# Finer DMA transposes of q and k, ten x buffers and attention further ahead in a fused attention and MLP kernel

## The chip, the cores and the metric

One core of a Trainium2 chip. The metric is the time of one execution on the device in microseconds (us), as the median of several runs. PE is the matmul engine, PEld its weight loads, DVE the vector engine, ACT the scalar engine, POOL the engine that issues the loads, SP the engine whose queue issues the DMA transposes and the stores.

## The reference

```python
def _attn_ref(q, k, v):                      # q, k, v: [8, 8, 576, 64]
    scores = scale * q @ k.T                 # per batch and head
    mask = (rel >= 0) & (rel < 128)          # sliding window, ALiBi bias
    attn = softmax(where(mask, scores + bias, -1e9))
    return attn @ v
def _moe_ref(x, w_in, w_out):                # x: [4608, 512]
    h = x @ w_in                             # [4608, 2048]
    return (h * cos(h)) @ w_out              # [4608, 512]
```

The output of the attention, with heads joined, is the `x` of the second part.

## The kernel before

Attention is cut into 72 units: per batch eight units (head pair `pr`, token half `G`) and a tail unit `t`. The second part is cut into nine chunks of 512 tokens. Each chunk has a first stage (64 matmuls of 512 columns, in two of the chunks 128 of 256) and a second stage, which from chunk 1 on is made of seven products instead of eight. Between the stages of chunk c, `QUOTA[c]` units of attention are worked.

```python
QUOTA = [9, 9, 11, 11, 9, 9, 5]
NX = 8                                        # x buffers
...
def dma_transposes(b):                        # batches 2 to 7, on the SP queue
    for which in ("q", "k"):
        fns = [ ...transpose of token blocks 0 to 3..., ...transpose of the tail block... ]
        op("sp", fns, r=[("nat", which, b % 2)] + ..., w=[("tr", which, b % 2)], ...)

def load_nat(which, src, b):                  # q or k of a batch, on the POOL queue
    op("pool", fns, r=[("tr", which, 0)] if b == 3 else [], w=[("nat", which, b % 2)], ...)

def tkeys(u):                                 # what the scores of a unit wait for
    keys = [("tr", w_, b % 2) for w_ in ("q", "k")] + [("ktail", b % 2)]
```

The `r=` of `load_nat` for batch 3 holds the q loads of that batch until the q transposes of batch 2 have landed, and the k loads likewise for k. Each finished x tile is transposed either by PE or, when its chunk is not the next one, by DMA from the SP queue:

```python
first = (S * u[0] + (512 if u[1] == "t" else 256 * u[2])) // CH
by_dma = first > phase + 1
```

A string `STARTS` holds a planned start for each operation, worked out beforehand; operations are sorted by it, and each engine runs its own in that order. Stores of the result go through four buffers `ob` and stand in the same SP queue as all transposes by DMA:

```python
op(("act", "dve"), ..., w=[("B", bank), ("ob", oi), ...])                      # PSUM to ob
op("sp", [lambda e: e.dma_start(out[row:row + 128, :], ob[oi])], r=[("ob", oi)], ...)   # the store
```

The softmax here doesn't subtract the row's maximum and nothing guards it: scores larger than these inputs give would overflow.

## Time and profile before

| | kernel before |
|---|---|
| median of the first 3 runs | 301.37 us (301.10 to 301.57) |
| the profiled run | 302.63 us, span 300.9 us |
| PE busy | 291.0 us of the span |
| PE idle from 20 to 290 us | 2.60 us |
| DVE, ACT, POOL busy | 80%, 70%, 32% |

The row to read first is the last but one: if PE is the bound, its idle time in the middle is all that a change of waits can win. The profile is of one run, and that run was 1.3 us slower than the median. The lines themselves stand in the prediction.

### The profile page before, as it was taken

The numbers are of one execution on the slowest core, as the hardware profiler recorded it, in microseconds if no ns is written. First come the engines' busy times: TensorE is split into PE (matmuls) and PEld (weight loads), VectorE is DVE, ScalarE is ACT, GpSimd is POOL, SyncE is SP. The second block draws the span as 40 slices with busy tenths as digits, with TensorE's granted clock in tenths as the row PEclk, the third lists the DMA queues.
The fourth block names the chain that finished last, engine by engine and source line by source line (L and its number), as shares of the span: only waits on it lengthen the run. The fifth ranks groups of instructions, "written<-read, shape, count | busy, mean of one in ns | idle before, by whom it ended". The sixth has DMA issues, their size and how long they took to land.

```text
span 300.9 us, 7105 instructions
## 1 busy us (share of the span) xinstructions
PE 291.0 (97%) x2905; PEld 200.6 (67%) x2925; DVE 240.5 (80%) x478; ACT 209.7 (70%) x300; POOL 95.2 (32%) x122
## 2 busy tenths in 40 slices
PE   7799999999999999999999989999999999999996
PEld 3568746547774687548888876568755855566685
DVE  4687678789977998899988879788978967685871
ACT  6787977498857788588768775778676945645432
POOL 7998230069966322760196004000000000000000
PEclk9999999999999999999999999999999999999999
DMA  7999999999999999999999999942304111120033
GB/s 140 181 199 210 206 166 174 140 167 172 172 132 138 173 153 163 145 193 140 184 114 126 148 128 137 170 87 64 98 21 105 46 27 52 37 75 32 0 124 122
DMA packets 148352, 38.09 MB, mean 127 GB/s; under 512 B 133984, under 2 KB 147040, under 8 KB 148320
## 3 DMA queue, kind: packets, MB, share of 16 engines
q0 software_dynamic: 99344, 18.10, 78.4%
q1 hardware_dynamic: 48976, 19.54, 37.9%
q8 instruction: 23, 0.38, 0.5%
q14 instruction: 9, 0.07, 0.1%
HBM read 36.70 MB, written 9.44 MB: 153 GB/s over the span
## 4 chain that ended last, share of the span: by engine, by line
PE 59%; DMA 21%; POOL 14%; SPq 3%; issue 2%; DVE 0%; ACT 0%; POOLq 0%; DVEq 0%; ACTq 0%
PE ps L768 27%; PE ps L909 26%; DMA qnat<-in_q_dram 8%; DMA knat<-in_k_dram 7%; POOL vp L329 4%; POOL qnat L339 4%; SPq L350 3%; DMA qt<-qnat 3%; DMA kt<-knat 3%; PE ps L538 3%; POOL knat L339 2%; PE ps L623 1%; PE ps L626 1%; POOL w_outb L367 1%; POOL w_inb L361 1%
## 5 line engine op out<-in xcount | busy, mean ns | idle before, releaser
L768 PE MATMUL ps<-xT,w_inb 128*128 128x512 bf16 (+1 forms) x556 | 125.2, 354 | 0.7
L774 ACT ACTIVATE cos<-ps,halfpi 128x512 f32<-128x512 f32 x128 | 82.4, 687 | 46.2 <-PE ps L768 34.8
L778 DVE TENSOR_TENSOR gT<-ps,cos 128x512 f16<-128x512 f32 x128 | 83.0, 686 | 21.6 <-ACT cos L774 21.1
L768 PEld LDWEIGHTS ps<-xT,w_inb 128*128 128x128 bf16 x576 | 55.2, 98 | 39.7 <-DVE xnat L679 0.8
L568 ACT ACTIVATE p<-ps 128x768 bf16<-128x768 f32 (+1 forms) x64 | 55.6, 917 | 9.3 <-PE ps L538 8.5
L329 POOL DMA_DIRECT2D vp<-in_v_dram x40 | 34.0, 871 | 61.8 <-PE ps L626 48.1
L909 PE MATMUL ps<-wsum,gT 128*128 128x256 f16 x256 | 50.8, 273 | 0.4
L592 DVE TENSOR_TENSOR p<-p,emask 128x512 bf16<-128x512 bf16 (+2 forms) x88 | 39.0, 471 | 4.0 <-ACT p L568 3.5
L909 PE MATMUL ps<-w_outb,gT 128*128 128x256 f16 x256 | 39.7, 273 | 0.1
L909 PE MATMUL ps<-wsum,gsum 128*128 128x256 f16 x256 | 37.2, 273 | 0.1
L339 POOL DMA_DIRECT2D qnat<-in_q_dram x30 | 25.4, 892 | 18.1 <-DMA qt<-qnat 17.3
L909 PEld LDWEIGHTS ps<-wsum,gT 128*128 128x128 f16 x256 | 24.2, 98 | 9.1 <-DVE ob L933 0.8
L909 PEld LDWEIGHTS ps<-w_outb,gT 128*128 128x128 f16 x256 | 24.5, 98 | 8.4 <-ACT ob L929 0.3
L339 POOL DMA_DIRECT2D knat<-in_k_dram x30 | 25.6, 919 | 8.5 <-issue 5.9
L909 PEld LDWEIGHTS ps<-wsum,gsum 128*128 128x128 f16 x256 | 24.7, 98 | 4.6 <-ACT qrows L929 0.2
L909 PE MATMUL ps<-w_outb,gsum 128*128 128x256 f16 x128 | 26.1, 273 | 0.1
L679 DVE TENSOR_TENSOR xnat<-ps,rec 128x512 bf16<-128x512 f32 x28 | 19.3, 690 | 1.3
L929 ACT ACTIVATE qrows<-ps 128x512 f32<-128x512 f32 (+1 forms) x18 | 9.9, 552 | 14.2 <-PE ps L909 14.1
L538 PE MATMUL ps<-qt,kt 64*128 64x128 bf16 (+1 forms) x320 | 18.4, 239 | 1.3 <-issue 0.9
L623 PE MATMUL ps<-vp,p 128*128 128x65 bf16 x256 | 18.0, 193 | 0.8 <-DVE xT L740 0.4
L623 PEld LDWEIGHTS ps<-vp,p 128*128 128x128 bf16 x256 | 15.6, 97 | 3.9 <-issue 1.1
L626 PE MATMUL ps<-vp,p 128*128 128x65 bf16 x192 | 16.9, 193 | 0.0
(81 smaller groups left out, 333.1 us busy)
## 6 DMA issues: line engine op xcount, KB each, us to landing
out_dram<-ob SPq DMA_DIRECT2D x32, 256.0 KB, 4.7
vp<-in_v_dram POOLq DMA_DIRECT2D x32, 128.0 KB, 10.0
qnat<-in_q_dram POOLq DMA_DIRECT2D x24, 128.0 KB, 13.0
knat<-in_k_dram POOLq DMA_DIRECT2D x24, 128.0 KB, 17.4
w_inb<-in_moe_w_in_dram POOLq DMA_DIRECT2D x4, 512.0 KB, 10.2
w_outb<-in_moe_w_out_dram POOLq DMA_DIRECT2D x4, 512.0 KB, 21.9
out_dram<-ob SPq DMA_DIRECT2D x8, 128.0 KB, 1.8
qrows<-in_q_dram POOLq DMA_DIRECT2D x1, 576.0 KB, 15.0
```

What stands on the lines that cost most here:

```text
L329: op("pool", [lambda e, t=t, rows=rows: e.dma_start(vp[b % 2][0:rows, t, :, 0:64], v[b, :, 128 * t:128 * t + rows, :].rearrange("h p d -> ...
L339: fns.append(lambda e, t=t, rows=rows: e.dma_start(nat[which][b % 2][0:rows, t, :, :], src[b, :, 128 * t:128 * t + rows, :].rearrange("h p ...
L538: ins = e.matmul(ps[:, banks[x], c0:c1], keys_ap(b, x, pr, kc), query_ap(b, x, pr, qb, 128 * nb), start=not added, stop=True, skip_group_c ...
L568: op("act", lambda e: e.activation(P[i][:, :, 0:hi], src_[:, :, 0:hi], ACTF.Exp, scale=0.125), w=held + [("P", i)], occ=920 if G else 691, ...
L592: op("dve", lambda e, p=p, m=m: e.tensor_tensor(p, p, m, ALU.mult), r=[("P", i), ("EM", h0), ("EM", h1)], w=[("P", i)] if n != 1 else [("P ...
L623: ins = e.matmul(o, P[i][:, x, d0:d0 + 128], V[:, kc, h, 0:65], start=True, stop=not two)
L626: ins = e.matmul(o, P[i][:, x, p0:p0 + 128], V[:, kc - 1, h, 0:65], start=False, stop=True)
L679: op("dve", lambda e: e.tensor_tensor(o, U[:, :, :, 0:64], rv[:, :, :, None].broadcast_to([128, 2, 4, 64]), ALU.mult), r=[("rec", n // 2 % ...
L768: op("pe", lambda e, kc=kc, c0=c0: e.matmul(ps[:, bank, c0:c0 + n], w_in[:, kc, 128 * fc:128 * fc + 128], xT[:, kc, (r0 + c0) % XR:(r0 + c ...
L774: op("act", lambda e: e.activation(cosb[ci][:, :], ps[:, bank, :], ACTF.Sin, bias=halfpi[:, 0:1]), r=["halfpi"], w=[("B", bank), ("cos", c ...
L778: op("dve", lambda e: e.tensor_tensor(gT[gi][:, fc, :], ps[:, bank, :], cosb[ci][:, :], ALU.mult), r=[("cos", ci)], w=[("B", bank), ("g", ...
L909: op("pe", lambda e, t=t, fc=fc, bk=bk: e.matmul(ps[:, bk, 256 * t:256 * t + 256], lhs(fc, t), rhs(fc), start=first and fc == 0 and (last ...
```

## The change

Its intent is to let the scores of a unit start when the q and k blocks that this unit reads have been transposed, instead of waiting for the whole batch; to work some attention earlier (two units move from the phase of chunk 5 into that of chunk 4, and two from the last phase into that of chunk 5), with two more x buffers for it; and to use other PSUM banks for one early group of transposes. All starts were planned anew. The core of the diff:

```diff
 STARTS = ( ...the whole packed order is replaced... )
-        NX = 8
+        NX = 10
-        QUOTA = [9, 9, 11, 11, 9, 9, 5]
+        QUOTA = [9, 9, 11, 11, 11, 9, 3]
 # load_nat
-            op("pool", fns, r=[("tr", which, 0)] if b == 3 else [], ...
+            op("pool", fns, r=[("tr", which, 0, "p", 1)] if b == 3 else [], ...
 # dma_transposes: one operation of two DMAs for q and one for k become
+            for part, (c0, c1) in enumerate(((0, 2), (2, 4), (4, 5))):
+                for which in ("k", "q"):
+                    ...
+                    op("sp", [lambda e, o=o, i=i: e.dma_start_transpose(o, i)], ...
+                       w=[("tr", which, b % 2, "p", part)], dma=f"tr{which}{b % 2}{part}", ...)
 # tkeys
+            if b >= BPE:
+                parts = {0: {"q": (0,), "k": (0,)}, 1: {"q": (1,), "k": (0, 1)},
+                         None: {"q": (2,), "k": (1, 2)}}[G]
+            keys += [("tr", w_, b % 2, "p", i) for w_ in ("q", "k") for i in parts[w_]]
 # transposes of q of batch 1 by PE
-                    qk_transposes(1, "q", 0, half, SB[2:4])
+                    qk_transposes(1, "q", 0, half, SB[0:2])
```

More of the change, by code (lines that the diff above doesn't have):

```diff
@@ L30 @@
 STARTS = (
-    "c-pO24RBP|72cOXa(x5(I4W)~i!PU!n68h_l0Nn)ci$#JvTT>Qh5<sb{46Q06ag_HP0@nHLTijMGE9d;#FQ$-pI~Q%qT-BFY"
-    "cW#GD1!*tv9_RN!730;7P7DBy<IjxyHU&ZC42Y0bI-l^obP<++_eaL+;Z(nNjm=Fn{E-hvv26ov#utlbwS5Rz**D4Fw`x*pT"
-    "UBV^`+(7ocZasXYy75rdI*~@V_gyWw)jG2H!=pWYA@ZG2>cuRv5@Gp1~`N9uu;Y?k8>az8(mA2LG}y8DnmDmXKv07aJt#!dG"
-    "b#T<xzIe5LQZkY(xYtI59Ro!-mSxEWTr8CvgIy<c2?HTnQ!iXs`~y*B9S7z<ffg|CyW=^i*+18UL~@&1aev~36X#RmzN9m|L"
-    "h%0hq4uNR*Te9$uty#ng)CCAJ(4T>9B33!wc6NG+o_j|YGbpG$)WnW3t#QL$Tub(~45lmS~VkM;6q-!h#Xs|qVQ?F;LQ&eUp"
@@ L36 @@
-    "8dP`6COh6EW2X=jSr<AJSf!WD_3$c9A@paOklWGUCbu)g`n3Kfq;x`WXN7NEo9XHPj%$TXf$2T?3WgK8U-wWc7Ef8`=obc?T"
-    "XdRv64G7j?$5+QSH3*~mT#-$tengJO$K#lWTGX>#O}1+GHZkZ>)346i3_dgP8=LJ&>7s7GRwBaQgT*zSE53MEB_DDr9FdU{j"
-    "0GLyUkFNcXK9KdhEYTfeHf`XtJC40y$X@F>{5Wr`25iI#`jW$oV?0mv^OM)HOgq?(UWG-nmX$3IpGSee{AEwh;T)tLM6|t2E"
-    "?<^rF9<=4>xF(cZWmu4#JYc(1aEe`APoOIExO=~M2<Q+^BAzSI1Rr?tim8eAXGfJHn5U{yu>`?oQfna`Ic1qF8NvYf3s(e1J"
-    "DA4)zHOAc-M4Scrk@ldEN6xvebYB{>~Y^`Iq{>5y)cD(<lGW}FpS((2C2b>RuR@c2}eXYiJXwmKaXTl+vl7A+!oY|a=%_)*P"
@@ L41 @@
-    "1HKXG3(v8R+{ny#JW{7TY(&?nyMvD{TR8pHc=?!gxBV@-U7ku8d-gn%-%`Ma16?JZ*8Z&y2Qo{At=e8jL_*xu%105=FM=di@"
-    "jnA99e}zUP+)|JRz6G;32H>^<Z&tiLW$^{JkqulP!<FHY1~6R>D^w!|49rxLW=oZAhLw>RNIUyQV5l|^S?>72F(5Tp&ca+RO"
-    "TIM9f%Oc$|r_Oq5<DLw`+?>zZ#95XkRjvZL{s1_2gKXI(n4TJCXWtE|Mx_n;IHhIKu-KOmc^PQJU?OD)K9Q;Ot&+;HAAEsw{"
-    "~b(%X+8w?`W&tC0X|K$U{kAOS0m19b#g<044~30(y59NS4iaiLd|gED*bkz0bHdWIUPUhZyV;AUs-f#PCRFuo5YHK4sv6LdH"
-    "6iPdjP0quU7v>xX_T-dgW@hiCHiqh4%XQ1?Hrouv=hbPFsH7cI_(+8m%!ka%deDKXhpUNwK8$?;V6P;k=S8w%tF9wg(w}O+$"
@@ L46 @@
-    "z$Dq_^iHPsQ7Go;6^DyH|CI-o!ynzh!?oTJN00M>oNqItta{zsFyr;t+m1#*cYTQ98VNNA5Q+8OdlQnBROj(ZT9q=A@ne075"
-    "M>%QM6sDr5DWGjNez{Vvdu`PXd8Q`&?z!e^5PN-wKg~1HS&NVV(LX{1#t(8>4cJlDlo?9)>F#(%W4ZW@hLIZxJ|oA)cR)Lv3"
-    "<F^llvG{Gd_C(Kvb&$rr3E=HH8V<?->O<UkuU$#=l|_aB6=92KI@Q)N-(wu14tXeCo-=OUBt6>7rNeGe8;Ra*w5#<`%&uCKr"
-    "eAypX`h9h&EAK~c-U&j$`Y5N-d6N)3D*e6{M_C!r&uRR?d3ZjME7nH7CExOhl&3M=F(SOd##QaFi?4ZrhFeM}Uw2T>+lcM=i"
-    "#3)8@$FAy88Q$$!$Kumn`Q!wVC3yM4FG7yKAt{_wq-`bZb;3At!%8Z@ZDn<Q*8C-fG2+Ypcf-E)h$=;uom1q}LC~NV(QFaI#"
@@ L51 @@
-    "crKL`<eP+T#J3kY<K`ogQFi`VvFu>l2gsR|+H7;5*AOelH$&uvQ=5oPL#zr9@Ba(kZ#(i-5j^?*9ctAw*JB>=&7b2A4c$q*e"
-    "9|4>FFa8F!Io(I-ukV-zGsZ}rXkI>?Z4Qvo$f7y=jUJe9C>Bm{%BO+u+hGvWTR6Hd=}jx88L$ihjqS;h}EZ{kw*BQgB0;>go"
-    "+Z~h$Dp()Ho@T5#Ji8h;))5XtPm+VtErQ@yo{U#f`(Hd;)1)Jn67ZT$K2oHny~YP<4^}%R)lToeTI56?+ji_;qXIDAL5Apy*"
-    "Q-9a6x#SRIN`_n}bfJ=lvxhv>BPJi<&vyY{I_B|}vBTw*Sj?OZn{1_eCV=wn7bXp7BqA)=k%WS$}6X<dd2=NX@8_{|JE0cRE"
-    "Lgib!=#r6AdZHbQXc%NxK=MLXhTla=X7B1Cjpv-V8?xD-2`U(z1l}8-j7w9XtCyS()y_?pBqM=QP-#O-J%ZWOo<5VztWi#=k"
@@ L56 @@
-    "U_H_-lK_Egl3*3&ttpYEp2D^%Qdyme3Zy`{7ML`4p?6R$ZYOYukA>0GN>sZHqjEU^>Oo2rHw|2BP$IOIKDW}^R7(xM3<IoP-"
-    "=9FDO{K3o{#DmnI@PPPhQ-T{OF=vD07_Nf9axVndqRQ}v!1Ph0P^mP6lip7XC#H@Xrr)&70i2HVM+m?zQLiedp<&j+O;VYmV"
-    "`b%+ScKLXIjs?!$W^bi#+hN>c+_+kE~MM&pTdm|E{QT%KUQ<Z~lRoX3Z;-W}luZb-IYxMb0-Utq!q)(j>=dt<lGVP?>xeNBB"
-    "0;p85<B#b%wKfG|<gINokgKw1W*7!0$#hu0aXc_XUm6v^pz;mFgzCFc6FAo4r3n<#Urzs6|Ez6XO8!@Qq@)HL~&#Foc>AE}*"
-    "D=KDverp(TBRYj`RJiCqJy9=+60KZdWwhh`^Rg%@xwcuCmKe!nuS?N;@zh)MF5-Fdf<@>SKRUj<k7uqhLnhsOvSE}KmTj^*I"
@@ L61 @@
-    "{P<X*2P*$Fu4UuWLa(cBbK?o@8Hq?RSZY-Y+{k`$nrL)oBa}&1KmsWM6d+Y~234u~juR@BuQIzE7?oGO5!Nlp+qWJ_Gl*qGr"
-    "Ah-Lw7z1>Zs}?S*&IRY?C}SvYAya4YTQk;cl|v)hfRIhp&&!n1cNwgFCJVU<op<HU&`N6BGPic29~x?(;kv!y!~eQ7Yu6F9z"
-    "I%!_rUk$`Z_xojy7U-?OLhA0j+~U<Hy=+P}RcHA#;wojzpu!MiQAa_iiM9V_lT`_gGh|;!;sXmMZwmqa4IMU%gEI)J!N<F^{"
-    "TskXRiAl^Q=E77`j&t)Eb;h$>NQ9H^t>hB4FklOV2P3iV^vBQ3@*drnkU8B`J^iisvIzPw>ii=A&)DQ%kjqsX?EZf)qfbE<v"
-    "%t_ZM_D~lVgH`@98Dny#KeK28(mp>4xYc154)kq8c&s>bwMeKY>^#-=2^tM)@jr{zAh6AkhRI92efBiY0E05o{&>Cv5UU>9v"
@@ L66 @@
-    "3RJ<n1J6bGDOuSzoGDvW%;5^=P>5~Yp=U?Wm=P9(W)6)zl_+(A%WOV~H4@%F?QUx3_r2imWCu9pPkf&lJ#6$wB!+Pzoldeq&"
-    "+iz$H9-$(Pu7LR&a(dk0l(UW"
+    "c-oy-4RllG8O}{x_<BY8{8S7d0prK*58+Zmy-SmR`DqJ;7`spq(ohj2{?%AEsQ5$WIN%^K=m7+OkX7Xr#!!?wr@+DKoEx*_a"
+    "1IEZZGvt`1%{grrUEHVa`)bwG^9;|>ODQT?|r|&_j%sueZLq4HEHO6GL|Z+szEg*1w(<*nKTHgfdu%If;M1Cy>uh}<Y_OXAz"
+    "wJ7JB8Gcs_mJY)5oWwkI~c<&%~6-SZW`ZAvgA{N9|)YdD;CgKdSaRPzR|3OM;q#&@+_YYct=*^C`XrHBpdMje_>ol`p9Af=;"
+    "7GVb5pa*&I)2Z%<y1r=TnA%tSh9A#Dp;%w}bypPoK(sr|s6vW&^RB%CjNCul+w3>R{;DfGs2;nK;ylp`<R+mqj$qiz<mvE_2"
@@ new lines @@
+    "4UIKrAJccZJ_miWnDDw<4Ef}LJ7*XP^a9*DVd>OBVT}Xa^zIu6t9@UqY?Z9(=XsVkj;R*^$_D55hTFRa~Ad%5>Iw=W5clXIp"
+    "#52qDjOR3JjB#~f?CMV8TZ5)As4U@1*nfz=2J}*sAPBv8F&4!7Sl_#+^<+BHBLkOSd-+jAKSy=G(*n%o0lL0MW><#eyu9-n+"
+    "i2+OR;Sw8t=K~2>6GZy#FcrAeSfYCa=M$4Q{9ER+ElZ&naE--TX(``wVAk7WSWtGA;XFQ@nqPFU)(2_o|+SF+;{~!^?lFvg5"
+    "2w3F!pg!ek==G;$j(Pm2XcH5;-NCxKhc&HK+;~8ywV|5#kWKvQ^rz8tP+8((nU3`8qK|Zs76m?kMCcr7v)oq6B^l<s}Sx$*$"
+    "ffCk)>oQO*owydR*?>3O@<B^1{oCexV~G7?mKid*Qu@KQU(1;LQzQH9jcydF`i8H~xx#HZ$5LCIWCAM5(^X(!i>Rgc}sB&I*"
@@ new lines @@
+    "7DvOIPrs~Q~1B}<i@QKQgilz1)?VlgNe!AaZ<@cX^Kism(Kg1NDDSUmWy0%J9O!Dlis;Y8T!fT@+o+*chkm+nh<Af2{{D_=X"
+    "t}Q+@_81!xW9A@y28WIN*n6J6yq!IJcLk0~g=WLB`i3W7u;2Zm6F#qVenCUh)1EKpxf+U=A_v9tZ1MPv&2_f<NJRE^?zbsLM"
+    "8d?xZ$<>kgpj(40w&-@i1PCYW+4ir6`BEmCcX=428Gc_T!>2WA-UHym472@8@d0Gng=WPrWS}Meu5xz0zoY%zF6}RM9uE!;a"
+    "^bH&RswW1}~$|+dKvHJfjxag~7jE_gQ2=UguavSJv*d-!X<vl#*rPyR5hb%%Vai;BB~}0<6JGz!|ok08{c+6X{>yXneiAIhN"
+    "n{_;K7E(Z1g8ishd>zR?odgPHUk!C@s#e5Md4O!~8nEyFF0G$@!<5`xFwV<Spqoo_9{5|$*~6lInnnA8#0SOyeDo5Bt6k1Po"
@@ new lines @@
+    "hOl<DWL}9Y~*Nsi2)w#UEq(r@Qq95Q#tE-QY*UFuP38T~MU+`ds@jD2-y<7<q3!lui_alTbc}BH|!RTHIQ^x0PArly1JeOd`"
+    "Z*R9dPS7ffYd^gOPcIW~b}z*bkHwRUMwbU}YPha~I7>#^10{9zv=h6FMpqE2h-gS_m&DrQO}|^QcTmk%zoYJx#m%RrEkUZM0"
+    "TL#f=H`n*$Wm3>gKmCXLEW}UupLRJCPK6?Gi1pjg+*jq(LF;l>;FsEv?B<=Y$>cjRxQ)VZfw&Q5wr}6jQW<AC0D$*j1X(7`*"
+    "mQ7Ifq6aq?J#RTuWwpKPp>Irh4yN7(ME7pT&fP_|FInF}@rW*Yt~L3HFuor<mfi@TWr|QtEyeShnyFwSC5`3JZHCts<0ICQW"
+    "X4I0}7#rIx@y$C2?;X_<qY@uacDEz$CT)8=&oTQ}GP;~HpZ1#uVM;v~{%+pLaivz<OY7XRknwuAl+ew-gG^@J8h4quqnY?xK"
@@ new lines @@
+    "^kGt=;5*?~e0U@TDE<5q-_^Iw6I=oeMiQR+{3aML7L=Z2jDuxA`f5c8j1YM(ISObg9sKQwWBMWWXhJ>1<*Y6(VGy)z`RvZX<"
+    "Jg5e3Q#{8NM#}hbP@RRp7y(W3he)i+@4Qv{6RF`hlPL4^1B@sZUI^N>c@G023*F;DS$22VA_>=cuV%Py1usxAW8RWR7p<(G_"
+    "c#evc@GdxQ&UP8+1H!*P}k5&j_F0eDsLDWd0{e}>}s$FZgtE*T|r(y^#<tZ`R`_T{KXu3WAhmDg=?eLu}0ow|M?j5a7|<o=q"
+    "uiw9}K)?-@X0}3LlJY+j+u98&hHd!hi+SH7(E&W_2sdjE3IP46?h(7eUfXz?ZoaJXIhV3XR2&iYWz~_{^Gy(6C+COEB4nTu7"
+    "phTE`nJt{U7<wVXIyFkz`kqe@`i9_>7sX5sZAqW2pMpOb1gsFiCyP4o<*7XBrkPiSZ*TFTuNmiQ^N-!@p!7?Lg3PsmnKE<t7"
@@ new lines @@
+    "dzEsXdnHPx^D{x+^_c5d}ZK}n)covcn4Z3RiaHt~&skQL+Y0#zh527FlArziaUBdK05!7%^Q{eT3k#QCD#kMo{z*P&)ofVSv"
+    ")u`7bjec@=$6j-E$30_93%@!wyW^Frt${gS{GX1c<$<f4pQ<LS+S;{h-WWfkyj7Z57eO77ZHLBxj+jKSIUOf4H9+Ll6H2KLA"
+    "{o}z<|F7L_p&6V$k)JnpfUrJDWWs%07tp#0QPVCXrE4fSbHP;OohC&YOB`LVTYgSDck*D(<f0~L8GBsE$&Z2xvhMTi{PXDq2"
+    "Ow4<-eC^IVA4Ym0QRNW4wf5>frS<)G0p?nl1ItfOdD3Ph=EEr@P=<<O|}DgWg9;6qvmI&4B+~n?i>}W4rg&3gW6>aev41=J^"
+    "Znbe2!qVT|nCPM6fK8SA+9%zni`IWn<=Y=83OPd2O_P`NfXo-SIVkaWWW_@-oyBqND5rhr4qJ}^zmC=lq7i6<g5ZIpC#MXS;"
@@ new lines @@
+    "sPecvcE_C>e9cUBWNx(@ML`%iW?aq}%+utv`=zRI_%7uforgk)1p}C#*K_&9jj96QLd^>Bh)zwc|md!oxzIv*QD7=7SiSe@%"
+    "TjJnfha$?%8N)DXWc+Z8mCkk_ZdBf5ya-wx<9A_6k=>usl}e@iF@;d(ymP|NonP*LuXZ`mvSDpSrR06gerWaFh;8O?BXooh="
+    "~5&5RXfOT6`5Jabt#Nw=sk5v!Wr072#sjeyV|;`W|+AFFq#@|GV*95P)M`&C`H4Zo1j8vt1K&4vo#ozRt|TDt*|P{2x<mlLv"
+    "N(y9QKh`p)>578oX~kgE9WoAdxK-kL_oVmOeOL!LJs3-B=Em&O0FQ3|U`(MIjv)er<3Ebo9JnuoWt@j*%$;ayN#x2XGW`<Ml"
+    "4u5^+E9jLXG%<jBk;102uoo<Y%8D;2ju9S0SO5z_|G64x`-2LcPz31*}eIc-r)wQdYxfNBpi{hP>?=~-=*Cup>6^kFK?NQnY"
@@ L68 @@
+    "4jf+t?Y(Xvw$*wx&Lv;$0JVXBnz_hkRum{QT`-Rf-Bd&;R(8R%W6*6rB2-ml4(!d?95dd-UJ6ieB-&#C17XGmOeoYhKrL^xZ"
+    "<9{SOn|=JI<SgG??!_bsmsw|{Y_q#NJwu=*4!`sj<Z?l6>2b-O7oJ8-y^+dwhg^;&2d|<`t37s7``rY_zF>GIH6QgX#gE$CK"
+    "y_4_JhJ|s{aP9+v_hCu7p9=k4Z7AL>Xzs9a{eIvX6nu&`=nIH&zB@dE|f*RFP=<`ymO>F^39aU#eHdEV0M!IA2{&inE"
 )
@@ L341, in load_nat @@
                     src[b, :, 128 * t:128 * t + rows, :].rearrange("h p d -> p h d")))
-            op("pool", fns, r=[("tr", which, 0)] if b == 3 else [], w=[("nat", which, b % 2)],
+            op("pool", fns, r=[("tr", which, 0, "p", 1)] if b == 3 else [], w=[("nat", which, b % 2)],
                dma=f"ldn{which}{b % 2}", occ=4400, lat=4500)
         def dma_transposes(b):
-            for which in ("q", "k"):
-                t = tr[which][b % 2][:, :].rearrange("p (c k t) -> p c k t", c=NBLK, k=NPAIR)
-                fns = [
-                    lambda e, t=t, which=which: e.dma_start_transpose(
-                        t[:, 0:4, :, :].rearrange("p c k t -> p (c k) t"),
-                        nat[which][b % 2][:, 0:4, :, :].rearrange("p c h d -> p (c h d)")),
-                    lambda e, t=t, which=which: e.dma_start_transpose(
-                        t[:, 4, :, 0:64],
-                        nat[which][b % 2][0:64, 4, :, :].rearrange("p h d -> p (h d)")),
-                ]
-                op("sp", fns, r=[("nat", which, b % 2)] + ([("ktail", b % 2)] if which == "k" else []),
-                   w=[("tr", which, b % 2)], dma=f"tr{which}{b % 2}", occ=2500, lat=4300)
+            for part, (c0, c1) in enumerate(((0, 2), (2, 4), (4, 5))):
+                for which in ("k", "q"):
+                    t = tr[which][b % 2][:, :].rearrange("p (c k t) -> p c k t", c=NBLK, k=NPAIR)
+                    src_ = nat[which][b % 2]
+                    if part < 2:
+                        o = t[:, c0:c1, :, :].rearrange("p c k t -> p (c k) t")
+                        i = src_[:, c0:c1, :, :].rearrange("p c h d -> p (c h d)")
+                    else:
+                        o = t[:, 4, :, 0:64]
+                        i = src_[0:64, 4, :, :].rearrange("p h d -> p (h d)")
+                    op("sp", [lambda e, o=o, i=i: e.dma_start_transpose(o, i)],
+                       r=[("nat", which, b % 2)] + ([("ktail", b % 2)] if which == "k" else []),
+                       w=[("tr", which, b % 2, "p", part)], dma=f"tr{which}{b % 2}{part}",
+                       occ=3150 if part < 2 else 1300, lat=1900 if part < 2 else 500)
         def load_w_in(u):
@@ L505, in tkeys @@
             keys = [("tr", w_, b % 2) for w_ in ("q", "k")] + [("ktail", b % 2)]
+            parts = {"q": (0, 1, 2), "k": (0, 1, 2)}
+            if b >= BPE:
+                parts = {0: {"q": (0,), "k": (0,)}, 1: {"q": (1,), "k": (0, 1)},
+                         None: {"q": (2,), "k": (1, 2)}}[G]
+            keys += [("tr", w_, b % 2, "p", i) for w_ in ("q", "k") for i in parts[w_]]
             if b < BPE:
```

## The prediction

> **What bounds the kernel now.** I read four views of the profile of before: the page (shares, slices, chain), the windows, the timeline of PE and of the sync queue, and the view of the tile `qt`. The page says that PE has almost no room:
>
> ```profile
> PE 291.0 (97%) x2905; PEld 200.6 (67%) x2925; DVE 240.5 (80%) x478; ACT 209.7 (70%) x300; POOL 95.2 (32%) x122
> PE   7799999999999999999999989999999999999996
> DMA  7999999999999999999999999942304111120033
> ```
>
> To see are the nines in PE from the third slice to the last but one, and that the DMA engines are as full until slice 26 (about 195 us) and nearly free after it. A busy PE could still be slow, so I looked in the chain of waits at long unbroken runs of one line:
>
> ```profile
> 156.73 6.44 PE ps L768 x59
> 285.60 12.41 PE ps L909 x112
> ```
>
> 6.44 us over 59 matmuls of 256 columns is 109 ns each; 12.41 over 112 is 111 ns. Elsewhere in the chain 19 matmuls of 512 columns take 4.10 us, 216 ns each. At these rates line 909 alone costs 896 x 0.111 = 99 us, line 768 448 x 0.216 + 128 x 0.109 = 111 us, lines 792 and 853 another 28 us: 238 us of the two dense products, which the change leaves alone. Then I asked for three stretches:
>
> ```profile
> 20.00:290.00 270.00, 267.40 (x2613) 184.18 (x2634) 224.58 (x430) 192.44 (x270) 76.73 (x92) 1.00 1.19 124
> 0.00:20.00 20.00, 15.59 (x221) 9.55 (x221) 12.75 (x43) 14.94 (x25) 18.42 (x31) 1.00 1.27 169
> 290.00:300.90 10.90, 8.00 (x74) 6.85 (x71) 3.17 (x7) 2.31 (x7) 0.00 (x0) 1.00 0.37 125
> ```
>
> The second figure is PE's busy time. In the 270 us of the middle PE is idle for 2.60 us. The head (4.41 us idle: first loads, warm-up) and the end (2.90 us: last eviction and store) are touched only through the packed order. So the change plays for about 2.6 us, 0.9% of 301.37. Some of that is not even real: 20 of the 576 matmuls of line 768 lack records, and most of the small gaps sit there.
>
> Where are the real ones? From successive matmul starts, minus the columns of the first at full rate, I find three of note after 20 us: about 0.44 us before 117.66, about 1.0 us before 179.16, and 0.3 us at 182.84, where the first stage of chunk 5 begins. The timeline of PE for the second, the chain for the first, and the timeline of the sync queue:
>
> ```profile
> 179.16 0.51 PE L538 MATMUL ps<-qt,kt 64*128 64x256 bf16 x8 [0.86 <-issue]
> ```
> ```profile
> 109.38 8.23 DMA kt<-knat
> 117.61 0.05 issue
> 117.66 0.50 PE ps L538 x8
> ```
> ```profile
> 152.15 6.69 SPq L350 DMA_TRANSPOSE kt<-knat  x1
> 158.88 1.31 SPq L353 DMA_TRANSPOSE kt<-knat  x1
> ...
> 165.42 6.00 SPq L350 DMA_TRANSPOSE qt<-qnat  x1
> 171.46 1.28 SPq L353 DMA_TRANSPOSE qt<-qnat  x1
> 172.84 9.07 SPq L753 DMA_TRANSPOSE xT<-xnat  x5
> ```
>
> The view says "issue" at 179.16 because it names no waiter's partner there. In the trace the q tail transpose issued at 171.46 lands at 179.07, 0.09 us before the scores of batch 6 start: that is the wait. The other is batch 4, whose k tail transpose lands at 117.61. For the rest I subtract the last landing of a batch's transposes from its first scores: batch 2 has 7.2 us to spare (64.63 to 71.84), batch 3 5.9 (98.13 to 104.05), batch 5 3.3 (144.56 to 147.87), batch 7 10.3 (199.89 to 210.21).
>
> **What the Trainium skill says.** (1) "Trainium Kernel Development and Optimization", Performance Expectations: matmul busy time is a poor measure since matmuls are pipelined; use the share of weight loads. Here PEld is 67%, so by that measure PE looks less full than by its 97%; the 109 to 111 ns of unbroken runs settle that PE is paced by columns, and that the idle figure is the room. (2) "DMA: Bandwidth & Descriptors", Issuing engines are not separate DMA queues: DMAs of different issuers share the same 16 engines and interleave. The trace agrees: the same k transpose takes the sync queue 6.69 us at 152.15 beside loads and 1.90 us at 195.06, after the last of them. (3) The same page, Queues, rings and completion order: each engine takes turns between the rows that have work, a packet at a time. No view shows single packets taking turns, but a slowdown to a third fits it.
>
> **The change part by part.** (a) Transposes in parts. Before: per batch one large and one tail transpose of q, and the same of k, 4 issues; every score waits for all of both. After: 6 issues, interleaved k, q over blocks 0-1, 2-3 and tail; the units of G 0 wait for the first pair only. 12 more issues over batches 2 to 7. A large one costs the queue 4.0 to 6.9 us for q and 1.9 to 6.8 for k, a tail about 1.3. If a half costs half, a batch still takes about 15 us of the queue (6.69 + 1.31 + 6.00 + 1.28 = 15.3 for batch 6). What it buys at batch 6: knat landed at 150.38, so two halves from about 152 are issued by 159 and land some 6 us later, near 165, against 179.07. The stall there goes: -1.0 us. At batch 4, taken alone, knat lands at 104.06, two halves end at about 110 and land at about 116, against 117.61: -0.4 us.
>
> (b) The order k before q, and the changed throttle. The loads of batch 3 wait for a q transpose of batch 2:
>
> ```profile
> 63.09 1.75 POOL L339 DMA_DIRECT2D qnat<-in_q_dram  x2 [17.34 <-DMA qt<-qnat]
> ```
>
> Before, that q is the first thing on the queue and starts when qnat has landed, at 49.24; it lands at 62.69. After, the loads wait for the second q part, fourth in line, behind a k part that can't start before knat lands at 53.92. The four large pieces took the queue 4.98 + 3.05 = 8 us as two; from 53.9 they end near 62 to 63 and land some 3 to 4 us later, about 66. The loads of batch 3 start 3 to 4 us later. The POOL issues run without a break from 63 to 84 and landings lag by 4.5 us at first and 22 us at the end, so the loads of batch 4 are limited by the DMA engines and inherit most of it: knat at about 107.5 rather than 104.06, and first parts at 119.5 rather than 116. The scores of batch 4 came at 117.66 with no slack. If they keep their place, PE waits there 2 us longer than before; if the new order puts them a few matmuls later, nothing. I can't read the packed order, and book half with care: +0.6 net of the gain in (a), instead of -0.4.
>
> (c) Quotas. Two pairs move earlier: two units of batch 6 into the fifth, two of batch 7 into the sixth, and the last attention has 3 units. The rule for how x gets transposed gives, counted by hand, 26 units in pairs by PE and 30 by DMA both before and after, plus 8 tails by DMA. So PE loses no transposes: its work is the same to the matmul. Ten units in a row by DMA is why there are ten x buffers; before, no wait for an x buffer shows among the waits, so the two more only keep that so. Value: 0 to -0.3 us, at 182.84, where the x transposes of chunk 5 queue behind the q transpose that ended at 172.74.
>
> (d) Other banks for the q transposes of batch 1. PE is idle for 0.08 us from 20 to 50: worth nothing.
>
> Sum: -1.0 (batch 6) +0.6 (batch 4) -0.2 (chunk 5) -0.2 (a new packed order mostly tuned to help) = -0.8 us: 300.6.
>
> **The rivals.** First, the delayed loads: the wait moves from transposes to loads, at batches 3, 4 and 5. For it: the DMA row is all nines until 195 us and batch 4 has no slack. Against: the parts return about as much as the delay takes, and batches 3 and 5 have 3 to 6 us. At its worst, 2 us at batch 4 and some at batch 5: 302.5 to 303.5. Second, the sync queue jams: stores, x transposes and 36 parts wait in one line, and a part that waits for its load holds back an x transpose, so that a chunk's first stage starts late. For it: chunk 5 already waits 0.3 us. Against: after 195 us the DMA share is below 0.4. It would give 301.5 to 302.5. Third, everything works and the order also fills the head: 2 us of the middle and 0.5 us of the head give 298.9. Fourth, it is hidden altogether, both short stalls being replaced by others of their size: 301.4.
>
> **Range and chances.** The best case is bounded by 2.6 us of idle time and a little of the head, so 298.8 is my low end. Faster by 2% would need 6.0 us, more than twice what the middle has: 1%. Slower by 2% needs 6 us of new PE idle time, three times my estimate of the delay at batch 4: 3%. Range 298.8 to 302.6, 96% within 2%.
>
> **What would show it.** Right: the same number of matmuls of lines 692, 730 and 768; PE busy again about 267 of the 270 us; no gap before the scores of batch 6; first k and q parts landing about 12 us before the tails. The loads of batch 3 starting at 66 rather than 63, and knat of batch 4 landing after 106, would show (b). Wrong if the loads do not move, if PE's idle time in the middle is over 5 us, or if any gap over 1 us ends at a landing of loads or x transposes; wrong in the other direction if PE's idle time in the head falls by over 1 us, since I gave the order almost nothing.

## More of the kernel before

Every run quoted here was classed fast.

The order of instructions on every engine does not follow from the source.

## The result, and the profile after

The changed kernel took 301.51 us (301.20 to 302.10, 6 runs) beside 301.50 us (301.10 to 302.11, 6 runs) for the kernel before. The ratio is 1.0001, with a 95% interval of 0.9987 to 1.0014. A ratio here is the mean time of one kernel's fast runs over that of the other's in the same rounds, so it is not quite the ratio of the medians. The result: the same time; it lies in the predicted range, 0.9 us above the predicted point.

The profiled run of the changed kernel took 301.20 us, the fastest of its six. Its page, and the three stretches of the windows (the second figure is PE's busy time, the next ones those of PEld, DVE, ACT and POOL):

```profile
PE 291.5 (97%) x2907; PEld 200.2 (67%) x2925; DVE 244.6 (82%) x485; ACT 206.4 (69%) x293; POOL 95.0 (32%) x122
PE   7889999999999999999999999999999999999996
DMA  7999999999999999999699999843133031202043
```
```profile
0.00:20.00 20.00, 16.04 (x221) 9.53 (x221) 12.81 (x44) 15.09 (x25) 15.35 (x27) 1.00 1.27 171
20.00:290.00 270.00, 268.78 (x2627) 184.98 (x2646) 230.11 (x438) 189.44 (x265) 79.62 (x95) 1.00 1.15 125
290.00:299.40 9.40, 6.65 (x61) 5.71 (x59) 1.70 (x4) 1.83 (x5) 0.00 (x0) 1.00 0.30 99
```

PE is idle for 1.22 us in the middle instead of 2.60, and the span is 299.4 us instead of 300.9. Some of both idle figures is bookkeeping: a matmul whose record is missing looks like a gap of 0.05 us or a little more. Of the first stage 20 matmuls lack their record in before and 18 here, which makes 1.1 us and 1.0 us; what is left is 1.5 us in before and 0.3 us here. The two waits are gone. These are PE's lines for the first scores of batches 4 and 6, from its timeline; neither has the bracket that told of idle time ahead of it:

```profile
117.62 0.50 PE L545 MATMUL ps<-qt,kt 64*128 64x256 bf16 x8
```
```profile
177.47 0.50 PE L545 MATMUL ps<-qt,kt 64*128 64x256 bf16 x8
```

So the profile says 1.5 us less and the times say nothing. Both are right. The profiled run of before was itself 1.1 us slower than the median of its six runs, the one of after 0.3 us faster than its own. (Time and span differ by 1.7 to 1.8 us in all of these runs, so nothing hides between them.)

The sync queue of the changed kernel shows that the packed order does not follow the order of the source. For batch 2 a q part is issued as soon as qnat has landed, and the load of batch 3 follows its landing at 58.2:

```profile
48.88 1.24 SPq L357 DMA_TRANSPOSE qt<-qnat  x1
54.13 4.98 SPq L357 DMA_TRANSPOSE kt<-knat  x2
59.15 3.07 SPq L357 DMA_TRANSPOSE qt<-qnat  x2
```
```profile
58.58 4.21 POOL L339 DMA_DIRECT2D qnat<-in_q_dram  x5 [12.59 <-DMA qt<-qnat]
```

As the load of batch 3 waits for the second q part and for no other, that first issue must be the second q part. It was planned first. The work of PE is the same, as predicted: 52 matmuls of x transposes and 576 weight loads of the first stage in both, 30 x transposes and 8 tails by DMA.

### The profile page after: what moved, and what is told of

It reads as the page before. It is cut to its first block, busy times and chain, and to the rows that moved or that the text cites. A ratio compares the mean times of both kernels' runs of the same rounds, so it can differ in the third digit from the quotient of the medians.

```text
span 299.4 us, 7150 instructions
## 1 busy us (share of the span) xinstructions
PE 291.5 (97%) x2907; PEld 200.2 (67%) x2925; DVE 244.6 (82%) x485; ACT 206.4 (69%) x293; POOL 95.0 (32%) x122
## 4 chain that ended last, share of the span: by engine, by line
PE 91%; DVE 3%; DMA 2%; ACT 2%; POOL 1%; issue 1%; POOLq 0%; DVEq 0%; ACTq 0%
PE ps L775 36%; PE ps L916 32%; PE ps L860 5%; PE ps L545 4%; PE ps L799 4%; PE ps L630 3%; DMA krows<-in_k_dram 2%; PE ps L633 2%; ACT p L575 1%; DVE p L599 1%; PE ps L483 1%; PE ps L699 1%; PE ps L617 1%; PE ps L619 1%; PE ps L535 1%
## 5 line engine op out<-in xcount | busy, mean ns | idle before, releaser
L916 PE MATMUL ps<-wsum,gT 128*128 128x256 f16 x256 | 49.1, 273 | 0.4 <-DVE ob L940 0.2
L916 PE MATMUL ps<-w_outb,gsum 128*128 128x256 f16 x128 | 26.8, 273 | 0.0
```

Source lines behind the costliest of these rows:

```text
L916: op("pe", lambda e, t=t, fc=fc, bk=bk: e.matmul(ps[:, bk, 256 * t:256 * t + 256], lhs(fc, t), rhs(fc), start=first and fc == 0 and (last ...
```

## The experiments

Each kernel was timed in five rounds beside the kernel before on the same chip, and its results were correct unless said. Where I built an order of my own, I took the planned starts of one of the two kernels and moved only the operations named.

**1. The kernel before again.** No edit. Theory N says that the waits belong to the slow run that was profiled; theory G says that they are usual and that the new order gives the same time back.

> The kernel before, unchanged, for a second profile. Theory N (the profile that I read was of a run at 302.63 us, 1.1 us above the median of the rest, and its two waits for transposes at 117.66 and 179.16 are not in a usual run): the time is within 0.4 us of 301.5, the profiled span is about 299.7 if its time is near 301.5, and PE's idle time from 20 to 290 us is 1.0 to 1.8 us instead of 2.6, with no gap over 0.5 us ahead of the scores of batch 6. Rival G (the waits are usual, the change takes them away and its new order gives the same 1.4 us back elsewhere): the gap of about 1.0 us ahead of the scores of batch 6 is there again, and the idle time is again about 2.6 us.

Measured: 301.90 us (301.20 to 302.65), ratio 1.000 (0.9976 to 1.0025). Its profile fell on the fastest run, 301.20 us. The window of the middle, and PE's timeline at the scores of batch 6:

```profile
20.00:290.00 270.00, 269.72 (x2644) 185.08 (x2641) 225.69 (x430) 192.45 (x271) 76.61 (x92) 1.00 1.18 125
```
```profile
177.49 0.27 PE L909 MATMUL ps<-wsum,gT 128*128 128x256 f16 x1
177.79 0.51 PE L538 MATMUL ps<-qt,kt 64*128 64x256 bf16 x8
```

The same program is idle for 0.28 us here, not for 2.60. Of the 1.0 us ahead of the scores of batch 6 some 0.2 us is left, of the 0.44 us at batch 4 some 0.14. A part of the other difference is bookkeeping: 2644 matmuls have records in this stretch against 2613. All weight loads have records, so I can lay the two profiles side by side by the starts of these: the slower run loses 0.26 us in the first 11 us, 0.30 us at the scores of batch 4 and 0.83 us at those of batch 6, 1.36 us in all, with the small differences elsewhere. Even in the fast run the last q transpose of batch 6 lands at 177.70, 0.09 us ahead of the scores: the whole transposes have no slack there. Theory N holds for the typical run; its idle time is even below the 1.0 to 1.8 us that I had expected. But the six times are three at 301.2 to 301.5 and three at 302.3 to 302.7, so the slow run is not rare either. In the 45 runs of the kernel before, those of this experiment counted, 11 took more than 302.2 us, two of them (303.35 and 304.32 us) at a mean clock of 0.994.

**2. Eight more matmuls ahead of the scores of batch 6**, in the kernel before.

```diff
+                if us[0] == (6, 0, 0):
+                    for _ in range(8):
+                        e.matmul(ps[:, slots[0][0], :], EM[:, 0, 0:128], ..., start=True, stop=True)
```

> The kernel before with 8 extra matmuls of 512 columns (8 x 0.216 = 1.73 us of PE) just ahead of the first scores of batch 6, where the first profile had PE wait 1.0 us. They sit in the same instruction group, behind the same wait, so they cost their full time whatever the wait is; what they test is whether PE is the bound at all. If PE bounds the whole: 301.5 + 1.7 = 303.2 us, ratio 1.0057. If some wait behind it (a load, ACT) had slack to give it back: under 302.6.

Measured: 303.73 us (302.89 to 305.27), ratio 1.0064 (1.0038 to 1.0090). The 1.73 us of work cost 0.64% of 301.9, that is 1.9 us, with an interval of 1.1 to 2.7 us. PE bounds the whole; no slack behind it gave the work back. Its profiled run, at 303.95 us above the median again, has a gap of 0.8 us ahead of the scores of batch 6, worked out from the matmul starts: a second slow run with a wait at that place.

**3. The parts alone**: the kernel before in its own order, with only the transposes in parts and the waits by part, and the three parts of q and of k at the places of the whole ones. The loads of batch 3 still wait for the last q part.

```diff
-            op("pool", fns, r=[("tr", which, 0)] if b == 3 else [], ...
+            op("pool", fns, r=[("tr", which, 0, "p", 2)] if b == 3 else [], ...
 # dma_transposes and tkeys as in the change; NX = 8 and QUOTA as before
```

> The kernel before in its own order, with its q and k transposes in the six parts and the waits by part; eight x buffers, old quotas, loads of batch 3 held until the last q part has been issued and landed. Theory N: same, 301.5 within 0.5 us. Rival G: the two waits (0.44 and 1.0 us) go and nothing gives them back: 300.1 us, ratio 0.995.

Measured: 301.05 us (300.83 to 301.22), ratio 0.9971 (0.9951 to 0.9991). Neither theory as I had put it: the gain, 0.29% or 0.9 us, is somewhat over half of what G asked for, and it is clear of zero. The interesting part is the spread, 0.4 us where the kernel before beside it spread over 2.2 us. Middle of its profile, of a run of 300.83 us:

```profile
20.00:290.00 270.00, 269.76 (x2643) 185.21 (x2640) 225.65 (x430) 192.47 (x272) 76.62 (x92) 1.00 1.16 125
```

It is idle for 0.24 us, as the fast run of before is for 0.28. The parts change little in a lucky run. In its profile the first parts of q and k of batch 6 have landed by 173.2, 4.2 us ahead of the scores. In none of the six runs did the time go past 301.22 us.

**4. The new order alone**: the changed kernel with whole transposes, each at the place where its first part had been.

> The changed kernel in its new order, quotas and ten x buffers, with the transposes whole again (two DMAs of one semaphore, all scores wait for all of a batch). Theory N: the whole transposes were no usual wait before, but the new order pulls batch 6 ahead by 1.6 us and two of its units by 20 us, so a little: 301.5 to 302.3 us. Rival G: the order is what costs, and without the parts nothing pays for it: 302.9 us, ratio 1.005.

Measured: 307.32 us (306.31 to 309.05), ratio 1.0184 (1.0151 to 1.0216). Worse than either theory allowed, and for neither reason. PE has one gap of 4.4 us, from 81.7 to 86.2, and no score waits in it. (All six runs have a mean clock of 0.988 to 0.994; in the profile it is 0.60 from 86 to 90 us, right after the gap.) DVE's timeline tells what it waited for:

```profile
85.42 0.69 DVE L931 TENSOR_TENSOR ob<-ps,krows 128x512 f32<-128x512 f32 x1 [4.00 <-DMA out_dram<-ob]
```

A second-stage result of chunk 1 could not leave its PSUM bank, because the `ob` buffer for it still held a tile of chunk 0. The store of that tile stood in the sync queue behind the whole q transposes of batch 3 (issued from 72.91, the second of them for 4.42 us) and went out at 78.77, to land at 85.4:

```profile
74.31 4.42 SPq L351 DMA_TRANSPOSE qt<-qnat  x1
78.77 0.58 SPq L863 DMA_DIRECT2D out_dram<-ob  x1
```

Experiment 9 takes this up.

**5. The changed kernel again, and 6. the parts alone again**, beside each other on one chip.

> The changed kernel, unchanged, beside the next ones on one chip. If its new order costs what the parts gain (theory O): 301.4 to 301.7 us, 0.4 us or more above the kernel with the parts alone. If the earlier difference (301.51 against 301.05) was one of chips (rival): equal to it within 0.2 us. The profile should show PE with less done at 20 us than the parts alone, 221 weight loads against 233, if theory O puts the loss into the head; if it varies from run to run, some number between.

> The parts alone in the order of before, a second time: 301.05 us within 0.25, all runs within 0.5 us of each other, where the kernel before spreads over 2 us. If the first result was chance: 301.5 and a spread like that of before.

Measured: 301.30 us (300.99 to 301.73), ratio 0.9981 (0.9957 to 1.0006), for the changed kernel; 301.14 us (300.91 to 301.65), ratio 0.9973 (0.9947 to 0.9999), for the parts alone. The two differ by 0.16 us, inside my 0.2, and their runs overlap: which of them is faster is not settled. Theory O, that the new order costs what the parts gain, is not borne out. The parts alone spread over 0.7 us here, more than the 0.5 us that I had expected; their profile fell on the slowest run, 301.65 us, and the 0.8 us between it and the profile of experiment 3 (300.83 us) are all lost in the first 11 us. The number of weight loads begun by 20 us is 221 and 228 in the two profiles of the changed kernel, 233 and 221 in those of the parts alone, 221 and 229 in those of before: the head varies by up to a dozen matmuls from run to run and tells the kernels apart in no way.

**7. The parts in the order of the source**, in the changed kernel: k before q, blocks 0-1, 2-3, tail, at the six places that the parts of each batch had.

> The changed kernel with each batch's six parts issued in the order of the source, k before q, blocks 0-1, 2-3, tail, at the six places in the queue that the parts had. My prediction took this order for granted; the packed order issues the second q part of batch 2 first. If step (b) of the prediction was right about what that order does: the loads of batch 3 start at 64 to 67 us instead of 58.6, knat of batch 4 lands after 101 instead of 96.0. For the time: by the prediction up to 2 us more (303.5) through the scores of batch 4; by the landings in the profile of the changed kernel, whose first parts of batch 4 land 9 us before the scores, nothing or up to 0.5 us: 301.5 to 302.0.

Measured: 304.80 us (304.02 to 307.23), ratio 1.0106 (1.0070 to 1.0143). The loads of batch 3 start at 63.16 instead of 58.58, a little earlier than predicted. But knat of batch 4 lands at 96.9, where the changed kernel had 96.0: the later start is not handed on. The time is lost elsewhere, in one gap of 4.1 us at 81.5, and it is the same store. The timeline of the sync queue, and the line of DVE:

```profile
64.94 1.25 SPq L356 DMA_TRANSPOSE qt<-qnat  x1
76.40 1.24 SPq L356 DMA_TRANSPOSE kt<-knat  x1
77.68 0.91 SPq L871 DMA_DIRECT2D out_dram<-ob  x1
```
```profile
84.91 0.69 DVE L939 TENSOR_TENSOR ob<-ps,krows 128x512 f32<-128x512 f32 x1 [3.63 <-DMA out_dram<-ob]
```

The queue works in order. The k part at its head waited until knat of batch 3 landed at 76.40, and the store behind it, ready since long before, waited with it. In the changed kernel the queue in the same stretch lets the store out between two q parts, before the k part that waits for knat:

```profile
69.01 1.18 SPq L357 DMA_TRANSPOSE qt<-qnat  x1
70.23 0.58 SPq L872 DMA_DIRECT2D out_dram<-ob  x1
70.85 1.40 SPq L357 DMA_TRANSPOSE qt<-qnat  x1
75.28 5.86 SPq L357 DMA_TRANSPOSE kt<-knat  x2
```

There it lands at 77.2, 4 us before DVE writes the buffer at 81.15.

In the profiled run the gap costs more than its length: it took 307.23 us, 5.7 us above 301.5. The windows show why; the third figure from the right is the granted clock:

```profile
78.00:82.00 4.00, 3.76 (x54) 2.82 (x50) 3.21 (x8) 3.26 (x5) 4.00 (x6) 1.00 1.90 147
82.00:86.00 4.00, 0.35 (x2) 0.28 (x3) 1.06 (x3) 1.05 (x2) 3.01 (x4) 0.77 1.82 196
86.00:90.00 4.00, 4.00 (x47) 3.00 (x45) 2.06 (x4) 0.39 (x1) 0.00 (x0) 0.50 1.66 113
90.00:94.00 4.00, 3.95 (x50) 3.11 (x49) 3.24 (x8) 2.84 (x3) 0.38 (x1) 0.88 1.88 156
```

After the gap PE works for 4 us at half its clock. (The mean clock of this run was 0.989, of the one in experiment 4 it was 0.994. It does not always come so: three of the six runs here, of 304.0 to 304.3 us, kept a mean clock of 0.999 or 1.0; the other three, of 305.3 to 307.2 us, had 0.989 or 0.994.) The Trainium skill says this in "TensorE: Matmul & The Clock Gate", What's actually happening: after one idle window of about 3.4 us the clock goes to 4/8, and it comes back after a busy one. The trace agrees, with a gap of 4.1 us and a granted clock of 0.50.

**8. Less PE work**: the changed kernel with one of the seven products of the second stage cut from 256 to 16 columns. Its output is wrong, which doesn't matter for the time.

```diff
-                            ps[:, bk, 256 * t:256 * t + 256], lhs(fc, t), rhs(fc),
+                            ps[:, bk, 256 * t:256 * t + (16 if name == "P3" else 256)], lhs(fc, t),
+                            rhs(fc)[:, 0:16] if name == "P3" else rhs(fc),
```

> The changed kernel with one of the seven products of the second stage (16 matmuls per chunk, chunks 1 to 8) cut from 256 to 16 columns; the result is wrong on purpose. It takes PE work away to see what stands right behind PE. Each of 128 matmuls should go from 0.110 us to between 0.04 and 0.06 (the weight load remains), so 128 x 0.05 to 0.07 = 6.4 to 9 us less PE. If PE bounds the whole and nothing is close behind: 293 to 295 us. If DVE (82% busy) or the loads (DMA full until 195 us) are close behind: half or less of it, 297.5 to 299 us, with new gaps on PE that end at DVE or at landings.

Measured: 297.75 us (297.31 to 297.82, 5 runs), ratio 0.9859 (0.9833 to 0.9886). Against 301.30 for the changed kernel of the same call, 3.5 us are saved, where PE's busy time fell by 8.3 us (from the 291.5 us of the changed kernel's profile to 283.2). The rest became waits. The middle, and two groups of PEld's waits (total us, times, longest):

```profile
20.00:290.00 270.00, 264.48 (x2657) 179.92 (x2676) 230.79 (x441) 190.56 (x267) 79.69 (x95) 1.00 1.17 126
```
```profile
PEld ps L698 <- DVE xnat L685: 3.1, 10, 0.6
PEld ps L915 <- DVE ob L940: 1.9, 5, 0.5
```

PE is idle for 5.5 us (about 0.9 us of it again missing records), much of it behind DVE. So PE is the bound, but by a few microseconds only; this is the second of the two cases that I had written down, with something close behind PE. I did not shift the order to suit the shorter product, so a new plan might save more.

**9. The new order alone, with the store first**: as experiment 4, with the q transposes of batch 3 planned just behind the last store of chunk 0 (those of k came behind it already).

> The same as the order alone (whole transposes in the new order), but with the transposes of batch 3 placed behind the last store of chunk 0 in the sync queue. If the 4.4 us wait of PE at 81.6 came only from that store, held behind the transposes, and the slower clock after it followed from the wait (theory S): 301.4 to 302.0 us, no PE gap over 1 us. If the scores need the parts in the new order (rival): still 303 us or more, with gaps ahead of scores of batches 4 or 6.

Measured: 301.23 us (300.97 to 301.46), ratio 0.9976 (0.9946 to 1.0005). Theory S holds: about 6 us of the 307.32 hung on that one store (the two were timed on different chips, each beside the kernel before), and the mean clock is back at 0.999 or 1.0. The sync queue:

```profile
66.73 0.70 SPq L863 DMA_DIRECT2D out_dram<-ob  x1
71.83 5.77 SPq L348 DMA_TRANSPOSE qt<-qnat  x1
77.64 1.28 SPq L351 DMA_TRANSPOSE qt<-qnat  x1
79.02 6.00 SPq L348 DMA_TRANSPOSE kt<-knat  x1
```

This run says one more thing. It has whole transposes, waits for the whole batch, and loads of batch 3 that start at 62.1; and it is not slower than the parts. The new order starts both transposes of batch 6 by 149.2, against 165.4 for q in the first profile of before, and the last lands at 158.8, 18.6 us ahead of the scores. A better place in the queue does what the parts do. Either takes the short waits away, and no run shows a gain of the second on top of the first.

**10. The source order, with the store first.**

> The same as the source order of the parts, but with the first k part of batch 3 behind that store. Theory S: 301.3 to 301.9 us although the loads of batch 3 still start near 63 and not at 58.6, so that the later loads by themselves (step (b) of the prediction) cost under 0.4 us. Rival, the later loads count: 302.5 us or more.

Measured: 301.88 us (301.08 to 302.89), ratio 1.0000 (0.9965 to 1.0036). The 3 us are gone, so the store was the cause here too. The loads of batch 3 start at 62.9 and knat of batch 4 lands at 98.0. The median is 0.65 us above that of experiment 9, whose loads start just as late, so the late loads do not explain it. Five of its six runs are above the slowest of experiment 9, so it is probably not chance; its cause stays open.

**11. The changed kernel with eight x buffers.** With `NX = 8` 191 operations would come before what they wait for; I moved each just behind it, which is no new plan.

> The changed kernel with eight x buffers instead of ten, each instruction that then comes too early moved back to just behind what it waits for (191 of 2730 are moved). Step (c) said that the buffers only keep a wait away. If the order needs ten: PE gains gaps ahead of second-stage or score matmuls in the fifth phase (170 to 200 us), 302 us or more. If eight would have done: 301.3 to 301.7.

Measured: 331.05 us (330.37 to 331.39, 4 runs), ratio 1.0961 (1.0920 to 1.1002); the profiled run has a mean clock of 0.969. The two large gaps on PE, of 13 and 8 us, end like this in the waits of the whole run (total us, times, longest):

```profile
PE ps L773 <- DVE xnat L684: 21.1, 2, 13.0
DVE xnat L684 <- DMA xT<-xnat: 14.5, 2, 9.5
```

DVE waits for an x buffer whose DMA transpose has not landed, and everything behind it in DVE's queue waits too. The new order can't be run with eight buffers without this loss, unless it is planned anew. What a plan made for eight would take is not shown: the kernel before is such a plan for its own quotas.

**12. The kernel before with ten x buffers.**

> The kernel before with ten x buffers and nothing else. No wait of before names an x buffer, so: equal to before within its interval (301.4 to 302.0, spread of 1 to 2 us as before). Faster by more than 0.5 us would say that x buffers held something back that the waits do not show.

Measured: 301.66 us (301.20 to 302.01), ratio 0.9989 (0.9959 to 1.0019): the same, as expected.

The times side by side:

| kernel | median us | fastest to slowest | ratio to before (95%) |
|---|---|---|---|
| before (first six) | 301.50 | 301.10 to 302.11 | |
| before (33 runs beside experiments 1 to 12) | 301.54 to 301.72 by call | 300.94 to 304.32 | |
| changed | 301.51, 301.30 | 300.99 to 302.10 | 1.0001, 0.9981 |
| parts alone | 301.05, 301.14 | 300.83 to 301.65 | 0.9971, 0.9973 |
| new order alone, store first | 301.23 | 300.97 to 301.46 | 0.9976 |
| new order alone | 307.32 | 306.31 to 309.05 | 1.0184 |
| parts in source order | 304.80 | 304.02 to 307.23 | 1.0106 |

The parts alone beat the kernel before by 0.3%, twice, with intervals that both end below 1, the second only just: without the run of 303.35 us at clock 0.994 beside it, its ratio would be 0.998. Against the changed kernel their lead is not resolved.

## Why the prediction was right or wrong

**The bound and the room: right.** PE bounds the kernel (experiment 2), its work is unchanged, and no result of a sound version lies more than 0.3% below before. The bound of 2.6 us on the gain was correct as a bound and too generous: a lucky run has 0.3 us, and 1.1 us of the 2.6 were missing records.

**Step (a), parts: right in mechanism, mis-sized.** The scores of batches 4 and 6 no longer wait; in the profile after, the last of the first q and k parts of batch 6 lands at 168.0, 9.5 us ahead of the scores (I had said near 165). The term that I booked at -1.0 us for batch 6, and -0.4 us for batch 4, came from a profile of a run at 302.63 us, while the median was 301.37. In the profile of a run at 301.20 us the two waits together are 0.3 us. The parts alone gained 0.8 to 0.9 us in the mean (0.27 to 0.29% of 301.9), partly because the runs above 302.2 us, 11 of 45 for before, did not occur in their 12. (They did not occur in the 12 runs of the changed kernel and the 6 of experiment 9 either; nor in the 6 of experiment 12, whose transposes are those of before, so six such runs prove little.) That the waits for transposes make these slow runs is supported by three profiles (1.0 us of wait at batch 6 in a slow run, 0.8 in another slow one, 0.2 in a fast one) and by laying two of them side by side (experiment 1); it is not shown for each run.

**Step (b), order and throttle: wrong.** I took the order of the source for the order of the queue, though the packed order was in front of me as a string that I could not read; I ought to have left the step open. The second q part of batch 2 goes first, and the loads of batch 3 start 4.5 us earlier than in before instead of 3 to 4 us later. Where the order is as I assumed (experiments 7 and 10), the loads start at 63, not at 66, and the second link of the step fails as well: knat of batch 4 lands at 97 to 98, not at 107.5. The 1.0 us that this step added at batch 4 (+0.6 instead of -0.4) was therefore no term at all. The sign that the first parts land some 12 us ahead of the tails failed with it: the k tail of batch 6 is the first of its parts to land, at 149.1.

**Steps (c) and (d): right for the buffers, the rest not separated.** The counts of transposes by PE and DMA are as predicted; ten buffers alone change nothing (experiment 12), and the new order needs them (11). The wait of 0.3 us before chunk 5, from which I booked 0.2 us, was no wait: the weight load at 182.95 has no matmul record in that profile, and in the profile of experiment 1, which has all records, the gap at this place is 0.08 us. The value of the quotas was not taken apart by any run, nor was the change of banks.

**The rivals.** "The sync queue jams" named the right danger and the wrong victim. It does not bite through x transposes and a chunk's first stage, but through a store whose buffer the next chunk needs. It does not bite in the changed kernel, where the store has 4 us to spare; it costs 3 to 6 us in two neighbours of it (4 and 7) and goes away when the store is put first (9 and 10). The fourth rival, "hidden altogether", came closest to the first measured ratio of 1.0001, but not by its mechanism: no new waits replaced the old ones, as PE's idle time in the middle of the profile after shows.

**The point.** -0.8 us was predicted, and +0.0 and -0.6 us (ratios 1.0001 and 0.9981, both with 1 inside their intervals) were measured in two sets of runs. Two wrong terms of opposite sign, a too large (a) and a (b) that did not exist, mostly cancelled. That the point came so close is therefore luck; what held is the bound on the gain.

## What to carry to other kernels

Before sizing a wait from a profile, compare the time of the profiled run with the median of the others: a wait of 1 us in a run that is 1.3 us slow may be the reason why that run is slow, and not what a change will win in the typical one. On an engine that issues DMAs in order, ask of each wait at the head of its queue what stands behind it; a store that waits behind a transpose can stop the matmuls through its buffer, and in both profiles with a gap of about 4 us (experiments 4 and 7) a slower clock followed it and cost again. Two remedies for one short wait, finer transposes and an earlier place in the queue, did not add up here.

## What the Trainium skill lacked or had wrong

- "TensorE: Matmul & The Clock Gate", Back-to-back issue gap, gives 131 ns for a sustained matmul of 512 columns in a stream with weight loads and says that the formula N/2.4 + 2.5 over-counts there. Here 19 matmuls of 512 columns in one stream took 216 ns each and 112 of 256 columns 111 ns each, which is the formula (216 and 109 ns).
- "DMA: Bandwidth & Descriptors", DMA Transpose (X-bar), gives no time that the issuing queue is held; the page counts a sequencer's cycles for a transpose only where it compares trn3 with earlier chips, and not beside other traffic. In the first profile of before one transpose of q or k held the sync queue for 1.2 us at the least and for 6.9 us beside running loads, and 2.4 to 13.7 us passed from its issue to its landing.
- No page spells out what decided experiments 4 and 7; "DMA: Bandwidth & Descriptors" says where a DMA's wait is served, at the issuing sequencer, but not what is held up behind it: a store that stands in an issuing queue behind a DMA whose wait is not yet met goes out late, however long its own data has been ready. There it cost 3 to 6 us of the whole kernel. Issuing the stores from another engine was not tried.
